# Maxima over partitions by a DRAM row, outputs in the raw weights' buffer, weights bounded and split by whole chunks

## Chip, core and metric

The kernel runs on one core of one Trainium2 chip. The metric is the device time of one execution in microseconds; of several runs of a kernel the median counts.

## What is computed

```python
# q, k, v: 8 batches x 8 heads x 576 positions x 64, float32
scores = scale * np.matmul(q, k.transpose(0, 1, 3, 2))
mask = pos[:, None] // 64 >= pos[None, :] // 64        # causal by blocks of 64
scores = np.where(mask, scores, -1000000000.0)
attn = np.exp(scores - np.max(scores, axis=-1, keepdims=True))
attn = attn / (np.sum(attn, axis=-1, keepdims=True) + 1e-09)
x = np.matmul(attn, v)                                 # then heads side by side: 4608 x 512
h = x @ w_in                                           # 512 x 2048
g = h * np.clip(h + 3.0, 0.0, 6.0) / 6.0
out = g @ w_out                                        # 2048 x 512
```

## The kernel before

Attention goes by slots: slot n is batch n // 4 and the pair of heads n % 4, so there are 32 of them. The second part (FFN below) goes by pieces of 384 or 192 tokens, 13 in all, and each piece by 16 rows f of 128 hidden features: `ffn1` makes the products `h` (24 half-width products where the piece has 384 tokens), ACT and DVE turn them into `r` and `g`, and three rows later `ffn2` adds the products `o` (18) to up to three accumulators of 128 tokens. After row 15 each accumulator is scaled into an `osb` tile and stored. Slots 0 to 3 and piece 0 work in float32. All others split each float32 operand into a high and a low float16 part and sum three products (`h`, `o`, `pv`) or two (`s`).

Splitting needs a power of two near the largest magnitude of the operand: per slot for q and k (`mb_q`), per batch for v, per chunk for the weights (8 chunks `c` of 256 hidden features, both matrices). `pow2_scale` finds it. Each partition first has its own bound (`mx`). With `exact`, PE spreads it along a row (`mt`), DVE takes the maximum (`dg`), PE spreads that over all partitions (`mb`), and DVE reads it (`am`, `pw`, `rs`). `v_max` does this for batch b before its slots (`vm1`), `w_max` for chunk c. `w_split` then writes high and low parts (`hi`, `lo`) in half chunks. The float32 form of chunk c lies where the split form of chunk c + 1 will be.

Weights arrive as 64-bit words in `raw` (one buffer of 4 KB per partition, besides parts of `ph` and other tiles) and are shortened to float32 with two `stage` tiles. `stage` has four buffers; `r` of pieces 1 to 12 and every `osb` take theirs from it too.

All instructions go through a `Recorder`, which is why they show one line in the profile (491). It notes what each reads and writes, and a planner orders them: each operation has a key (a due time, from tables such as `AT` for slots and `FT` for pieces, less `ADV` for attention on PE), each engine takes the ready operation with the lowest key, and readiness and costs are the planner's own estimates. Where `scaled` names several engines ("AVP"), the planner picks one. The engines then run their lists in that order, waiting where data is late. DMAs are all issued by SP, in one list: loads, stores, and transposes (`qkT`, `pT`) that turn split operands for PE. What stands behind a waiting DMA on SP waits too.

Of the kernel before, what the change touches and what calls it, by code (L numbers as in the profile page):

```python
# [25 lines left out]
U = 1.592
AS = (6.899, 12.918, 18.225, 24.115)
AL = 17.759
PV0 = 2.584
TA, TR, PR = 2.701, 5.502, 1.15  # L30
QR = 2.616
PVA, PVB = 1.013, 0.991
# [11 lines left out]
QL = -3.431
VL = -2.484
W0, WD = 16.803, 2.29
S0, SD = 55.334, 4.109
M0, MD = 36.221, 7.195
RT = (29.488, 39.58, 49.409, 59.423)
RS, RL, VL1 = 2.209, 24.843, 24.11  # L50
VM0, VMX = 49.529, 0.186
AT = ((4, 86.25), (6, 123.23), (8, 163.76), (9, 178.32), (10, 200.46), (12, 251.25), (14, 297.48), (15, 319.97), (16, 344.82), (24, 581.69), (32, 825.86))
FT = ((0, 34), (1, 120), (2, 165.28), (3, 233.86), (4, 274.28), (5, 355.06), (7, 504.5), (10, 755.22), (13, 989.58))
UNI = False
QP = 0.558
VP = 0.387
BLK = 64
EXPONENT_BITS = 0x7F800000

# [19 lines left out]
        return call  # L79


ADV = {("tensor", "a"): 99.24}
# [412 lines left out]
def kernel(  # L495
# [65 lines left out]
    def pow2_scale(mx, n, nm, to=None, exact=False):  # L561
# [8 lines left out]
        if exact:  # L570
            pt_ = ps_s.tile([P, 512], F32, tag="s", name=f"mt_{nm}")
            nc.joint = "mt", nm
            for h in range(2):
                wide = mx[:, h % n:h % n + 1].to_broadcast([P, BLK])
                nc.tensor.matmul(pt_[h * BLK:(h + 1) * BLK, :P], wide, ident, start=True, stop=True)
            nc.joint = None
            dg = sm.tile([P, n + 1], F32, tag=f"dg{n}", name=f"dg_{nm}")
            nc.vector.tensor_reduce(dg[:, n:], pt_[:, :P], axis=AX.X, op=ALU.max)
            nc.vector.tensor_scalar_mul(dg[:, :n], ident[:, :(n - 1) * BLK + 1:BLK], dg[:, n:])
            mx = dg[:, :n]  # L580
        ps = ps_s.tile([P, 512], F32, tag="s", name=f"mb_{nm}")
        nc.joint = "mb", nm
        for h in range(2):
            nc.tensor.matmul(ps[h * BLK:(h + 1) * BLK, :n], ones[:, :BLK], mx, start=True, stop=True)
        nc.joint = None
        nc.vector.tensor_scalar_max(am, ps[:, :n], TINY)
# [52 lines left out]
    def w_load(w, c, half):  # L639
# [35 lines left out]
            op0=ALU.logical_shift_left, op1=ALU.bitwise_or,  # L675
        )

    def w_max(c):

        acc = sm.tile([P, 2, 2], F32, tag="wacc", bufs=2, name=f"wacc{c}")  # L680
        for wi, w in enumerate("io"):
            for half in range(2):
                c32 = w_f32(w, c, half)
                ab = ffp.tile([P, WC], F32, tag="stage", bufs=NST_B, name=f"ab{w}{c}_{half}")
                ab = ab.rearrange("p (r l n) -> p r l n", r=c32.shape[1], l=2)
                nc.scalar.activation(ab, c32, AF.Abs, accum_out=acc[:, wi, half:half + 1])
# [4 lines left out]
    def w_split(c):

        rs = rsio[:, c]
        for wi, w in enumerate("io"):
            for half in range(2):
                c32 = w_f32(w, c, half)
                part = w_part(w, c, half)
                hi, lo = (part[:, :, i].rearrange("p r (l n) -> p r l n", l=2) for i in range(2))
# [829 lines left out]
```

## Time and profile before

| | before |
|---|---|
| median of 3 runs | 985.28 us (984.22 to 986.99) |
| profiled execution, its time | 982.83 us |
| profiled execution, its span | 981.0 us |
| granted TensorE clock | 0.999 |
| PE busy | 964.2 us (98%) |
| DVE busy | 756.4 us (77%) |
| ACT busy | 696.5 us (71%) |

The profile page gives busy time by engine. The view by stages gives it for stretches of the span (us from its start); the view of waits says for which instruction an engine stood idle and who released it. PEld is the loading of weights into PE, which overlaps the products. A line of groups gives count, busy time, mean ns of one, and idle time before it.

### The profile page before, as it was taken

How to read it: one execution, taken by the hardware profiler on the slowest of the kernel's cores; microseconds unless marked ns; L12 is line 12 of the kernel's file. 1: busy time of each engine (PE TensorE's matmuls, PEld its weight loads, DVE VectorE, ACT ScalarE, POOL GpSimd, SP SyncE). 2: the span in 40 equal slices, each digit the busy share in tenths (PEclk: the TensorE clock that was granted, in tenths of full speed). 3: DMA queues.
4: the chain of work that ended last, by engine and by line, in shares of the span. 5: the costliest groups of instructions: out<-in, count | busy, mean ns of one | idle time of the engine just before them, and what ended most of it. 6: DMA issues, size and time to landing. Idle time of an engine off the chain costs nothing.

```text
span 981.0 us, 29087 instructions
## 1 busy us (share of the span) xinstructions
PE 964.2 (98%) x11754; PEld 722.9 (74%) x11754; DVE 756.4 (77%) x2081; ACT 696.5 (71%) x1840; POOL 28.3 (3%) x109
## 2 busy tenths in 40 slices
PE   8999999999999999999999999999999999999998
PEld 6655447877778867777777677777777777777776
DVE  6889998999989999999999898899886432332331
ACT  6899789778778888888878788787775433333332
POOL 3012000000000000000000000000000000000000
PEclk9999999999999999999999999999999999999999
DMA  6966689899898899898899898786664200000000
GB/s 141 277 204 223 159 154 178 169 183 189 155 173 148 149 175 157 170 162 148 161 186 177 151 188 156 132 164 131 108 133 77 36 34 1 1 33 1 34 2 33
DMA packets 414199, 128.91 MB, mean 131 GB/s; under 512 B 403184, under 2 KB 403440, under 8 KB 414064
## 3 DMA queue, kind: packets, MB, share of 16 engines
q1 hardware_dynamic: 414064, 127.05, 66.5%
q8 instruction: 92, 1.51, 0.6%
q14 instruction: 43, 0.35, 0.1%
HBM read 45.09 MB, written 9.44 MB: 56 GB/s over the span
## 4 chain that ended last, share of the span: by engine, by line
PE 58%; DVE 6%; DMA 2%; ACT 1%; issue 1%; DVEq 0%; ACTq 0%
PE o L491 25%; PE h L491 25%; PE s L491 4%; PE pv L491 4%; DMA pT<-ph 2%; DVE st L491 1%; DVE phl L491 1%; DVE ph L491 1%; DVE r L491 1%; DVE g L491 1%; DVE qks L491 1%; DVE vhl L491 0%; ACT p L491 0%; DVE x L491 0%; ACT r L491 0%
## 5 line engine op out<-in xcount | busy, mean ns | idle before, releaser
L491 PE MATMUL h<-x,win 128*64 128x384 f16 (+3 forms) x4790 | 440.7, 319 | 4.4 <-DVE r L491 4.4
L491 PE MATMUL o<-wout,g 128*64 128x512 f16 (+2 forms) x3424 | 432.3, 383 | 0.0
L491 PEld LDWEIGHTS <-win 128*64 128x64 f16 x4608 | 296.1, 110 | 62.5 <-issue 6.5
L491 PEld LDWEIGHTS <-g 128*64 128x64 f16 x3264 | 219.2, 110 | 91.6
L491 ACT ACTIVATE r<-h,eg,sh 128x192 f32<-128x192 f32 (+1 forms) x240 | 134.1, 580 | 115.2 <-PE h L491 110.8
L491 DVE SCALAR_TENSOR_TENSOR r<-r,eg,h 128x384 f32<-128x384 f32 (+1 forms) x192 | 110.3, 575 | 132.0 <-ACT r L491 131.3
L491 ACT ACTIVATE p<-s,st,esc 128x64 f32<-128x64 f32 (+1 forms) x280 | 163.1, 586 | 13.6 <-DVE ph L491 7.3
L491 DVE SCALAR_TENSOR_TENSOR g<-r,g 128x384 f16<-128x384 f32 (+1 forms) x192 | 99.5, 519 | 34.1 <-ACT g L491 33.3
L491 DVE TENSOR_REDUCE st<-s 128x1 f32<-128x64 f32 (+1 forms) x280 | 119.2, 446 | 6.9 <-PE s L491 6.1
L491 ACT ACTIVATE g<-r 128x384 f16<-128x384 f32 (+1 forms) x157 | 77.4, 494 | 59.2 <-DVE r L491 58.7
L491 PE MATMUL s<-qkT 128*64 128x64 f16 (+7 forms) x1120 | 101.8, 287 | 1.9 <-ACT p L491 1.3
L491 PEld LDWEIGHTS <-vhl 128*64 128x64 f16 x1680 | 74.0, 110 | 13.5 <-issue 4.1
L491 PEld LDWEIGHTS <-qkT 128*64 128x64 f16 x1120 | 62.0, 110 | 23.5 <-issue 7.6
L491 PE MATMUL pv<-pT,vhl 128*64 128x192 f16 (+2 forms) x1680 | 74.4, 233 | 1.9 <-DMA pT<-ph 0.9
L491 DVE SCALAR_TENSOR_TENSOR ph<-p,st,ph 128x256 f16<-128x256 f32 (+2 forms) x168 | 66.5, 444 | 0.1
L491 DVE SCALAR_TENSOR_TENSOR phl<-p,st,phl 128x512 f16<-128x512 f32 (+1 forms) x84 | 62.8, 789 | 0.3 <-ACT phl L491 0.3
L491 ACT ACTIVATE st<-st,esc 128x1 f32<-128x1 f32 (+2 forms) x127 | 36.8, 291 | 34.3 <-DVE st L491 32.9
L491 ACT ACTIVATION_READ_ACCUMULATOR p<-s,st,esc 128x1 f32 x280 | 55.0, 196 | 0.0
L491 ACT ACTIVATE ph<-p,st 128x64 f16<-128x64 f32 (+5 forms) x106 | 43.2, 450 | 15.8 <-DVE st L491 14.2
L491 DVE SCALAR_TENSOR_TENSOR qks<-qk,rs_q,qks 128x576 f16<-128x576 f32 x56 | 44.5, 807 | 0.1
L491 ACT ACTIVATE qks<-qk 128x576 bf16<-128x576 f32 x56 | 37.8, 677 | 0.3 <-DMA qkT<-qks 0.3
L491 ACT ACTIVATE x<-pv 128x192 f16<-128x192 f32 (+1 forms) x56 | 20.3, 363 | 11.5 <-PE pv L491 10.0
(150 smaller groups left out, 847.0 us busy)
## 6 DMA issues: line engine op xcount, KB each, us to landing
out_dram<-osb SPq DMA_DIRECT2D x35, 256.0 KB, 2.7
vnat<-in_v_dram SPq DMA_DIRECT2D x64, 128.0 KB, 3.0
qk<-in_q_dram SPq DMA_DIRECT2D x28, 288.0 KB, 3.4
qk<-in_k_dram SPq DMA_DIRECT2D x28, 288.0 KB, 4.3
rawi<-in_moe_w_in_dram SPq DMA_DIRECT2D x8, 512.0 KB, 4.5
rawo<-in_moe_w_out_dram SPq DMA_DIRECT2D x8, 512.0 KB, 4.7
ph<-in_moe_w_in_dram SPq DMA_DIRECT2D x6, 512.0 KB, 4.8
ph<-in_moe_w_out_dram SPq DMA_DIRECT2D x6, 512.0 KB, 4.0
```

What stands on the lines that cost most here:

```text
L491: getattr(eng, method)(*args, **kw)
```

## The change

Six edits go together. `pow2_scale` has a second way (`far`) for chunks 3 to 7 and batches 1 to 7: the partitions' bounds are stored to a row in DRAM, read back with the row repeated on every partition (`al`), and reduced by DVE. `w_max` takes one sum of magnitudes over a whole chunk of a matrix in place of the larger of two sums over halves, and the scale of `g` leaves two more powers of two for that. `w_split` works on whole chunks, on ACT and DVE alone. The first two `osb` tiles of a piece share one tile with tag `raw`; the third stays in `stage`. The last `osb` is scaled and stored in two halves, stored by SP and ACT. k of slot 0 is loaded by ACT. The planner's tables are new.

```diff
-AT = ((4, 86.25), (6, 123.23), (8, 163.76), (9, 178.32), (10, 200.46), (12, 251.25), (14, 297.48), (15, 319.97), (16, 344.82), (24, 581.69), (32, 825.86))
+AT = ((4, 86.25), (6, 123.58), (8, 163.76), (9, 178.32), (10, 199.99), (12, 251.29), (13, 269.94), (14, 285.67), (15, 306.89), (16, 332.72), (24, 569.88), (32, 807.78))
+WFAR, VFAR = 3, 1
...
-ADV = {("tensor", "a"): 99.24}
+ADV = {("tensor", "a"): 19.74}
...
-            if self.on_chip(a):
+            if self.on_chip(a) or a.tensor.name.startswith("dr_"):
...
-    E_G = 2.0 ** -27
+    E_G = 2.0 ** -25
...
+    drp = ctx.enter_context(tc.tile_pool(name="dr", bufs=2, space=bass.MemoryType.DRAM))
...
+        if exact and far:
+            row = drp.tile([n, P], F32, tag=f"row{n}", name=f"dr_row_{nm}")
+            nc.sync.dma_start(row.rearrange("n p -> p n"), mx)
+            al = sm.tile([P, n, P], F32, tag="al", bufs=1, name=f"al_{nm}")
+            nc.sync.dma_start(
+                al.rearrange("p n x -> p (n x)"),
+                row.rearrange("n p -> (n p)").rearrange("(o x) -> o x", o=1).to_broadcast([P, n * P]),
+            )
+            nc.vector.tensor_reduce(am, al, axis=AX.X, op=ALU.max)
+            nc.vector.tensor_scalar_max(am, am, TINY)
...
     def w_max(c):
-        acc = sm.tile([P, 2, 2], F32, tag="wacc", bufs=2, name=f"wacc{c}")
+        acc = sm.tile([P, 2], F32, tag="wm", name=f"wm{c}")
         for wi, w in enumerate("io"):
-            for half in range(2):
-                c32 = w_f32(w, c, half)
...
-                nc.scalar.activation(ab, c32, AF.Abs, accum_out=acc[:, wi, half:half + 1])
...
+            c32, _ = w_whole(w, c)
...
+            nc.scalar.activation(ab, c32, AF.Abs, accum_out=acc[:, wi:wi + 1])
+        pow2_scale(acc, 2, f"w{c}", (pwio[:, c], rsio[:, c]), exact=True, far=c >= WFAR)
...
-                nc.scaled(hi, c32, rs[:, wi:wi + 1], "AVP")
...
+            nc.scaled(hi, c32, rs[:, wi:wi + 1], "AV")
...
-            vscale[b] = pow2_scale(m1, 1, f"v{b}", exact=True)
+            vscale[b] = pow2_scale(m1, 1, f"v{b}", exact=True, far=b >= VFAR)
...
-                nc.sync.dma_start(
+                (nc.sync if n or not s else nc.scalar).dma_start(
...
-            o = ffp.tile([P, DM], F32, tag="stage", bufs=NST_B, name=f"osb{pc}_{t}")
+            if t == 0:
+                pair = ffp.tile([P, 2, DM], F32, tag="raw", bufs=1, name=f"osb{pc}")
+            o = pair[:, t] if t < 2 else ffp.tile([P, DM], F32, tag="stage", bufs=NST_B, name=f"osb{pc}_{t}")
...
+            if pc == NPC - 1 and t == nt - 1:
+                for h, e in enumerate((nc.sync, nc.scalar)):
+                    cs = slice(h * DM // 2, (h + 1) * DM // 2)
+                    nc.scaled(o[:, cs], a[:, cs], so[:, t:t + 1], "AV")
+                    e.dma_start(rows[:, cs], o[:, cs])
+                continue
```

What it does to the order, at three places. SP's list at slot 17, where batch 5's maximum falls in the new order; before, first:

```order
L491 DMA vnat3_103<-in_v_dram 64x2x64
L491 DMA_TRANSPOSE pT17_1_1378<-phl17_6_1386 128x8x128
L491 DMA_TRANSPOSE pT17_1_1378<-phl17_7_1387 128x8x128
L491 DMA_TRANSPOSE pT17_1_1378<-phl17_8_1388 128x10x128
L491 DMA_TRANSPOSE pT18_0_1397<-ph0_87 128x8x128
```

And now:

```order
L495 DMA vnat3_105<-in_v_dram 64x2x64
L495 DMA dr_row_v5_1481<-vm1_5_1477 128x1
L495 DMA_TRANSPOSE pT17_1_1339<-phl17_6_1347 128x8x128
L495 DMA_TRANSPOSE pT17_1_1339<-phl17_7_1348 128x8x128
L495 DMA_TRANSPOSE pT17_1_1339<-phl17_8_1349 128x10x128
L495 DMA al_v5_1482<-dr_row_v5_1481 128x128
L495 DMA_TRANSPOSE pT18_0_1360<-ph0_89 128x8x128
```

The row's store stands ahead of the three transposes of slot 17 and the broadcast read behind them. On DVE, `am_v5` then stands 13 rows behind `vm1_5`.

ACT's list where piece 2 ends and piece 3 has begun, before (`osb2_1` went to DVE):

```order
L491 ACTIVATE r3_2_955<-h3_2_954,eg_625,sh1_792 128x192
L491 ACTIVATE osb2_0_958<-o2_0_806,so2_957 128x512
L491 ACTIVATE g3_2_956<-r3_2_955 128x192
L491 ACTIVATE p11_6_1029,st11_2_1024<-s11_2_1_0_1027,st11_2_1024,esc11_939 128x448
L491 ACTIVATE p11_8_1030,st11_2_1024<-s11_2_1_0_1027,st11_2_1024,esc11_939 128x64
L491 ACTIVATE osb2_2_960<-o2_2_808,so2_957 128x512
L491 ACTIVATE p11_8_1030,st11_2_1024<-s11_2_1_1_1028,st11_2_1024,esc11_939 128x512
L491 ACTIVATE r3_3_973<-h3_3_972,eg_625,sh1_792 128x192
L491 ACTIVATE st11_2_1024<-st11_2_1024 128x3
L491 ACTIVATE g3_3_974<-r3_3_973 128x192
L491 ACTIVATE phl11_7_1032<-p11_7_1026,st11_2_1024 128x4x128
L491 ACTIVATE r3_4_980<-h3_4_979,eg_625,sh1_792 128x192
```

And now:

```order
L495 ACTIVATE r3_2_936<-h3_2_935,eg_605,sh1_783 128x192
L495 ACTIVATE vhl12_1033<-vnat2_104,rs_v3_1014 128x5x128
L495 ACTIVATE g3_2_937<-r3_2_936 128x192
L495 ACTIVATE osb2_939<-o2_1_797,so2_938 128x512
L495 ACTIVATE osb2_2_940<-o2_2_798,so2_938 128x512
L495 ACTIVATE p11_6_991,st11_2_986<-s11_2_1_0_989,st11_2_986,esc11_900 128x448
L495 ACTIVATE r3_3_948<-h3_3_947,eg_605,sh1_783 128x192
L495 ACTIVATE p11_8_992,st11_2_986<-s11_2_1_0_989,st11_2_986,esc11_900 128x64
L495 ACTIVATE p11_8_992,st11_2_986<-s11_2_1_1_990,st11_2_986,esc11_900 128x512
L495 ACTIVATE st11_2_986<-st11_2_986 128x3
L495 ACTIVATE r3_4_953<-h3_4_952,eg_605,sh1_783 128x192
```

The outputs stand at much the same place; of the three only `osb2_2` is still a tile of `stage`, and the `r3` tiles that follow it come from there too.

SP's list at the end of attention, before (slots 30 and 31 are the last):

```order
L491 DMA_TRANSPOSE qkT31_2124<-qks31_2118 128x27x128
L491 DMA_TRANSPOSE pT30_0_2106<-ph1_88 128x18x128
L491 DMA_TRANSPOSE pT30_1_2141<-phl30_6_2149 128x8x128
L491 DMA_TRANSPOSE pT30_1_2141<-phl30_7_2150 128x8x128
L491 DMA_TRANSPOSE pT30_1_2141<-phl30_8_2151 128x10x128
L491 DMA_TRANSPOSE pT31_0_2160<-ph0_87 128x8x128
L491 DMA_TRANSPOSE pT31_0_2160<-ph1_88 128x18x128
L491 DMA_TRANSPOSE pT31_1_2177<-phl31_6_2185 128x8x128
L491 DMA_TRANSPOSE pT31_1_2177<-phl31_7_2186 128x8x128
L491 DMA_TRANSPOSE pT31_1_2177<-phl31_8_2187 128x10x128
L491 DMA out_0_dram<-osb9_0_2052 128x512
```

And now:

```order
L495 DMA out_0_dram<-osb9_2025 128x512 x2
L495 DMA out_0_dram<-osb9_2_2026 128x512
L495 DMA_TRANSPOSE pT30_1_2085<-phl30_6_2093 128x8x128
L495 DMA_TRANSPOSE pT30_1_2085<-phl30_7_2094 128x8x128
L495 DMA_TRANSPOSE pT30_1_2085<-phl30_8_2095 128x10x128
L495 DMA_TRANSPOSE pT31_0_2103<-ph0_89 128x8x128
L495 DMA_TRANSPOSE pT31_0_2103<-ph1_90 128x18x128
L495 DMA_TRANSPOSE pT31_1_2127<-phl31_6_2135 128x8x128
L495 DMA_TRANSPOSE pT31_1_2127<-phl31_7_2136 128x8x128
L495 DMA_TRANSPOSE pT31_1_2127<-phl31_8_2137 128x10x128
L495 DMA out_0_dram<-osb10_2157 128x512 x2
```

The last eight transposes of attention stood ahead of piece 9's outputs and now stand behind them. In PE's list 4334 of 21630 rows stood behind the last `pv` product, and now 3134 of 21599 do.

More of the change, by code (lines that the diff above doesn't have):

```diff
@@ L24 @@
 WY = 27
[L26 to L32, printed above, removed]
+U = 1.625
+AS = (6.639, 12.914, 19.786, 24.055)
+AL = 10.368
+PV0 = 1.9
+TA, TR, PR = 2.701, 5.748, 1.464
+QR = 1.086
+PVA, PVB = 1.108, 1.726
 PHS = 18
@@ L38 @@
 EVR = 3
-EVP = 4
+EVP = 0
 PRO = True
 MEM = 0
+BIASV = 261.576
+WFAR, VFAR = 3, 1
 NMIN = 64
[L44 to L51, printed above, removed]
-AT = ((4, 86.25), (6, 123.23), (8, 163.76), (9, 178.32), (10, 200.46), (12, 251.25), (14, 297.48), (15, 319.97), (16, 344.82), (24, 581.69), (32, 825.86))
-FT = ((0, 34), (1, 120), (2, 165.28), (3, 233.86), (4, 274.28), (5, 355.06), (7, 504.5), (10, 755.22), (13, 989.58))
+QL = -2.821
+VL = -1.472
+W0, WD = 21.694, 2.383
+S0, SD = 59.569, 3.454
+M0, MD = 31.889, 6.545
+RT = (29.11, 39.473, 49.187, 59.325)
+RS, RL, VL1 = 1.999, 24.929, 36.728
+VM0, VMX = 83.864, 0.17
+AT = ((4, 86.25), (6, 123.58), (8, 163.76), (9, 178.32), (10, 199.99), (12, 251.29), (13, 269.94), (14, 285.67), (15, 306.89), (16, 332.72), (24, 569.88), (32, 807.78))
+FT = ((0, 34), (1, 120.0), (2, 165.17), (3, 233.57), (4, 272.17), (5, 348.85), (6, 404.53), (7, 499.08), (10, 740.5), (11, 837.37), (13, 980.62))
 UNI = False
-QP = 0.558
-VP = 0.387
+QP = 0.67
+VP = 0.437
 BLK = 64
@@ L97 @@
     LOADS = 95.0
-    BIAS = {"vector": 250.0, "gpsimd": 500.0}
     EDGE = 0.0
@@ L108, in __init__ @@
         self.adv = ADV
+        self.BIAS = {"vector": BIASV, "gpsimd": 500.0}
         for n in self.NAMES:
@@ L116, in box @@
     def box(a):
+        if not Recorder.on_chip(a):
+            return 0, 1, 0, 1
         sz = mybir.dt.size(a.dtype)
@@ L535 @@
     E_X = 2.0 ** -14
-    E_G = 2.0 ** -27
+    E_G = 2.0 ** -25
     C_EXP = (D ** -0.5) * 2.0 ** -28
     C_H = 2.0 ** -28
-    C_O = 2.0 ** -15 / 6.0
+    C_O = 2.0 ** -17 / 6.0
     TINY = 1e-18
@@ L559, with pow2_scale @@
     padded = []
-    def pow2_scale(mx, n, nm, to=None, exact=False):
+    def pow2_scale(mx, n, nm, to=None, exact=False, far=False):
         if to:
@@ L569, in pow2_scale @@
         am = sm.tile([P, n], F32, tag=f"am{n}", name=f"am_{nm}")
-        if exact:
-            pt_ = ps_s.tile([P, 512], F32, tag="s", name=f"mt_{nm}")
-            nc.joint = "mt", nm
+        if exact and far:
[8 more added lines that the diff above has]
+            nc.vector.tensor_scalar_max(am, am, TINY)
+        else:
+            if exact:
+                pt_ = ps_s.tile([P, 512], F32, tag="s", name=f"mt_{nm}")
+                nc.joint = "mt", nm
+                for h in range(2):
+                    wide = mx[:, h % n:h % n + 1].to_broadcast([P, BLK])
+                    nc.tensor.matmul(pt_[h * BLK:(h + 1) * BLK, :P], wide, ident, start=True, stop=True)
+                nc.joint = None
+                dg = sm.tile([P, n + 1], F32, tag=f"dg{n}", name=f"dg_{nm}")
+                nc.vector.tensor_reduce(dg[:, n:], pt_[:, :P], axis=AX.X, op=ALU.max)
+                nc.vector.tensor_scalar_mul(dg[:, :n], ident[:, :(n - 1) * BLK + 1:BLK], dg[:, n:])
+                mx = dg[:, :n]
+            ps = ps_s.tile([P, 512], F32, tag="s", name=f"mb_{nm}")
+            nc.joint = "mb", nm
@@ L573, in pow2_scale @@
             for h in range(2):
-                wide = mx[:, h % n:h % n + 1].to_broadcast([P, BLK])
-                nc.tensor.matmul(pt_[h * BLK:(h + 1) * BLK, :P], wide, ident, start=True, stop=True)
+                nc.tensor.matmul(ps[h * BLK:(h + 1) * BLK, :n], ones[:, :BLK], mx, start=True, stop=True)
             nc.joint = None
-            dg = sm.tile([P, n + 1], F32, tag=f"dg{n}", name=f"dg_{nm}")
-            nc.vector.tensor_reduce(dg[:, n:], pt_[:, :P], axis=AX.X, op=ALU.max)
-            nc.vector.tensor_scalar_mul(dg[:, :n], ident[:, :(n - 1) * BLK + 1:BLK], dg[:, n:])
@@ L580, in pow2_scale @@
[L580 to L586, printed above, removed]
+            nc.vector.tensor_scalar_max(am, ps[:, :n], TINY)
         nc.vector.tensor_scalar(
@@ L676, in w_load, with w_whole @@
         )
+    def w_whole(w, c):
+        if w == "i":
+            part = win[:, c]
+            c32 = win[:, c + 1].bitcast(F32) if c + 1 < NCH else None
+        else:
+            part = wout[:, 2 * c:2 * c + 2]
+            c32 = wout[:, 2 * c + 2:2 * c + 4].bitcast(F32) if c + 1 < NCH else None
+        if c32 is None:
+            t = flat(xb[2 if w == "i" else 3], F32)[:, :2 * WC]
+            c32 = t.rearrange("p (r l n) -> p r l n", r=part.shape[1], l=2)
+        return c32, part
     def w_max(c):
-        acc = sm.tile([P, 2, 2], F32, tag="wacc", bufs=2, name=f"wacc{c}")
+        acc = sm.tile([P, 2], F32, tag="wm", name=f"wm{c}")
         for wi, w in enumerate("io"):
-            for half in range(2):
-                c32 = w_f32(w, c, half)
-                ab = ffp.tile([P, WC], F32, tag="stage", bufs=NST_B, name=f"ab{w}{c}_{half}")
-                ab = ab.rearrange("p (r l n) -> p r l n", r=c32.shape[1], l=2)
-                nc.scalar.activation(ab, c32, AF.Abs, accum_out=acc[:, wi, half:half + 1])
-        m = sm.tile([P, 2], F32, tag="wm", name=f"wm{c}")
-        nc.vector.tensor_reduce(m, acc, axis=AX.X, op=ALU.max)
-        pow2_scale(m, 2, f"w{c}", (pwio[:, c], rsio[:, c]), exact=True)
+            c32, _ = w_whole(w, c)
+            ab = ffp.tile([P, WC], F32, tag="stage", bufs=NST_B, name=f"ab{w}{c}")
+            ab = ab.bitcast(BF16).rearrange("p (r l n) -> p r l n", r=c32.shape[1], l=2)
+            nc.scalar.activation(ab, c32, AF.Abs, accum_out=acc[:, wi:wi + 1])
+        pow2_scale(acc, 2, f"w{c}", (pwio[:, c], rsio[:, c]), exact=True, far=c >= WFAR)
     def w_split(c):
@@ L694, in w_split @@
         for wi, w in enumerate("io"):
[L695 to L698, printed above, removed]
-                nc.scaled(hi, c32, rs[:, wi:wi + 1], "AVP")
-                nc.vector.scalar_tensor_tensor(
-                    lo, c32, rs[:, wi:wi + 1], hi, op0=ALU.mult, op1=ALU.subtract
-                )
+            c32, part = w_whole(w, c)
+            hi, lo = (part[:, :, i].rearrange("p r (l n) -> p r l n", l=2) for i in range(2))
+            nc.scaled(hi, c32, rs[:, wi:wi + 1], "AV")
+            nc.vector.scalar_tensor_tensor(
+                lo, c32, rs[:, wi:wi + 1], hi, op0=ALU.mult, op1=ALU.subtract
+            )
     gs = []
@@ L1338, in ffn2_ @@
             n, half = min(w - t * P, P), w - t * P < P
-            o = ffp.tile([P, DM], F32, tag="stage", bufs=NST_B, name=f"osb{pc}_{t}")
+            if t == 0:
+                pair = ffp.tile([P, 2, DM], F32, tag="raw", bufs=1, name=f"osb{pc}")
+            o = pair[:, t] if t < 2 else ffp.tile([P, DM], F32, tag="stage", bufs=NST_B, name=f"osb{pc}_{t}")
             oc = o[:, :DM // 2] if half else o
             ac = a[:, :DM // 2] if half else a
+            rows = out[row + t * P:row + t * P + n]
+            if pc == NPC - 1 and t == nt - 1:
[4 more added lines that the diff above has]
+                continue
             nc.scaled(oc, ac, so[:, t:t + 1] if pc else 1.0 / 6.0, "AV")
-            rows = out[row + t * P:row + t * P + n]
             if half:
@@ L1431 @@
         t = RT[n]
-        at(t - QR, qk_load32_rest, n, lead=RL - QR)
-        at(t - QR, qk_prep32, n, 1)
+        at(t - max(QR, 0.0), qk_load32_rest, n, lead=RL - max(QR, 0.0))
+        at(t - max(QR, 0.0), qk_prep32, n, 1)
         at(AS[3] + 0.1 + 0.1 * n, v_max, n)
```

## Prediction

> **What bounds the kernel now.** I read the engine sums first, then the stages, then who waited for whom. The page:
>
> ```profile
> span 981.0 us, 29087 instructions
> PE 964.2 (98%) x11754; PEld 722.9 (74%) x11754; DVE 756.4 (77%) x2081; ACT 696.5 (71%) x1840; POOL 28.3 (3%) x109
> ```
>
> The view by stages (length, then busy us of PE, PEld, DVE, ACT, POOL):
>
> ```profile
> 0.00:20.00 20.00, 15.36 (x103) 12.24 (x104) 13.12 (x41) 12.81 (x42) 7.41 (x32) 1.00 0.65 147
> 60.00:120.00 60.00, 60.00 (x411) 29.50 (x409) 59.14 (x170) 52.38 (x129) 10.24 (x10) 1.00 0.70 195
> 120.00:280.00 160.00, 156.58 (x2172) 116.64 (x2170) 152.01 (x455) 134.00 (x372) 2.59 (x16) 1.00 0.93 167
> 280.00:360.00 80.00, 76.83 (x1220) 61.52 (x1213) 70.31 (x209) 66.53 (x186) 1.21 (x8) 1.00 0.94 166
> 360.00:740.00 380.00, 378.86 (x4980) 295.27 (x4978) 345.50 (x949) 305.64 (x830) 4.84 (x32) 1.00 0.85 154
> 740.00:970.00 230.00, 229.58 (x2542) 175.26 (x2539) 81.01 (x158) 86.36 (x172) 0.00 (x0) 1.00 0.10 22
> ```
>
> PE is never idle for long, and from 740 on it works alone: DVE is at 81 of 230. So whatever product is taken off PE anywhere earlier lets the last FFN products start earlier, one for one, while PE stays fed. PE's idle time is the other thing to win: 4.6 us at the start, 3.4 in 120:280, 3.2 in 280:360, 1.1 in 360:740, 0.4 after. DVE is nearly full in 120:280 (152 of 160), so a wait put on DVE there is the danger. The waits (total, times, longest):
>
> ```profile
> PE h L491 <- DVE r L491: 4.4, 3, 2.0
> PE pv L491 <- DMA pT<-ph: 0.9, 2, 0.5
> ACT r L491 <- DMA out_dram<-osb: 3.8, 1, 3.8
> DVE vmax L491 <- DMA vnat<-in_v_dram: 1.4, 3, 0.6
> ```
>
> **The products removed.** A maximum over partitions is mt, then dg on DVE, then mb, am. The timeline of PE at batch 2's:
>
> ```profile
> 201.04 0.41 PE L491 MATMUL mt_v<-ident,vm 128*64 128x128 f32 x4
> 201.26 0.68 PE L491 MATMUL h<-x,win 128*64 128x384 f16 x6
> 202.72 0.26 PE L491 MATMUL mb_v<-dg_v,one 128*64 128x1 f32 x4
> 202.81 1.17 PE L491 MATMUL h<-x,win 128*64 128x384 f16 x12
> ```
>
> Busy times overlap, so I take the step from one start to the next: 0.22 for mt, 0.09 for mb, 0.31 together. Twelve of them go (chunks 3 to 7, batches 1 to 7): -3.7. Ends: 0 if PE only waits instead, and -8.0 by busy time (12 x 0.67). The steps say -3.7. DVE loses a reduction and a product over dg and gains a reduction over al: about even, 0.
>
> **The outputs' buffer.** Where piece 2 ends, its three osb tiles sit in the four stage buffers that r needs too:
>
> ```profile
> 289.24 1.51 SPq L491 DMA_DIRECT2D out_dram<-osb  x3
> 293.07 0.51 ACT L491 ACTIVATE r<-h,eg,sh 128x192 f32<-128x192 f32 x1 [3.84 <-DMA out_dram<-osb]
> 293.61 0.41 DVE L491 SCALAR_TENSOR_TENSOR r<-r,eg,h 128x192 f32<-128x192 f32 x1 [3.14 <-ACT r L491]
> 294.08 1.18 PE L491 MATMUL h<-x,win 128*64 128x192 f16 x24 [2.03 <-DVE r L491]
> 298.83 0.68 PE L491 MATMUL s<-qkT 128*64 128x256 f16 x8 [1.09 <-ACT p L491]
> ```
>
> ACT stood 3.84 us for the store, PE 2.03 right behind it and 1.09 for ACT's backlog. In the ACT order of before the second r after the last osb (r3_4) takes the first osb's buffer. With one osb left in stage, counting four buffers round, that is r3_6, two products h and two o later (1.18 of h alone each), and the store has landed by then. -3.1; ends 0 (the stall comes back elsewhere) and -3.8 (all of ACT's stand). The pair buffer is free: raw weights are long split, and pieces end tens of us apart.
>
> **The start.** k of pair 0 is issued by ACT beside q on SP:
>
> ```profile
> 0.73 0.99 SPq L491 DMA_DIRECT2D qf<-in_q_dram  x2
> 1.76 1.02 SPq L491 DMA_DIRECT2D qf<-in_k_dram  x2
> 5.37 0.56 DVE L491 TENSOR_SCALAR qkf<-qt 64x384 f32<-64x384 f32 x1 [3.01 <-ACT qkf L491]
> 5.80 0.49 ACT L491 ACTIVATE qkf<-qt 128x384 f32<-128x384 f32 x1 [0.47 <-PE qt L491]
> 6.39 2.74 PE L491 MATMUL sf<-qkf 128*128 128x128 f32 x8 [0.63 <-ACT qkf L491]
> ```
>
> k comes 1.0 earlier, its copy (ending 6.29) is no longer last, DVE's half of q (ending 5.93) is: -0.4. Ends 0 and -1.0. The table load that ACT has at the start moves behind its DMAs and ends long before 4.85.
>
> **The end.** The last tile's copy is halved over ACT and DVE and stored by two queues:
>
> ```profile
> 976.05 1.98 ACT L491 ACTIVATE osb<-o,so 128x512 f32<-128x512 f32 x3 [4.60 <-PE o L491]
> L491 ACT ACTIVATE osb<-o,so x28: 472/687/710, 203.2 to 977.3; 128x512 f32<-128x512 f32 x27, 128x256 f32<-128x256 f32 x1
> DMA to landing us min/median/max: 2.0/2.7/5.0
> out_dram<-osb SPq DMA_DIRECT2D x4, 64.0 KB, 2.8
> ```
>
> A copy of 256 columns took 0.47 for 0.69, and a store of 64 KB lands no sooner than one of 256 KB: -0.2. Ends 0 and -0.4.
>
> **Weights by whole chunks.** ACT saves 16 sums and 16 starts, DVE 14 to 16 starts; eight copies leave POOL for ACT and DVE:
>
> ```profile
> L491 ACT ACTIVATION_READ_ACCUMULATOR abi<-win 128x1 f32 x14 | 2.9, 210 | 0.0
> L491 POOL TENSOR_SCALAR win<-win,rsio 128x512 f16<-128x512 f32 x5 | 5.5, 1103 | 34.8 <-PE h L491 14.3 <-DVE win L491 10.7 <-DVE rsio L491 9.9
> ```
>
> ACT gains at least 16 x 0.21 = 3.4 and takes most of eight copies: about even. All of it lies in 60:120 and just after, beside a PE that was busy 60.00 of 60. 0; ends -1 and +1. Should that cover go, DVE (59.14 of 60) is late next.
>
> **The new order.** The order changes everywhere. Its largest move: behind the last pv product stood 4334 of PE's rows, now 3134. A row f of FFN is 84 such rows (24 h and 18 o products, each with its load) and takes 3.9 us in the chain of waits:
>
> ```profile
> 967.53 1.95 PE h L491 x24
> 965.59 1.94 PE o L491 x18
> ```
>
> 1200/84 x 3.9 = 56 us: attention ends that much later beside PE's work, so DVE's 345.5 of 380 thin out to about 84% (345.5 + 56 x 81/230, over 436). At most the 1.1 us of 360:740 can go. The 3.4 idle in 120:280 are dealt anew: 0 to double. I take -1.0; ends -4.5 and +3.4.
>
> **The round trip through DRAM.** It adds 24 DMAs on SP: a row written, a wait for its landing on SP, a broadcast read; DVE waits for that at am. Tightest of the batches is 5: between row and read stand three transposes on SP, and 13 rows of DVE stand between vm1 and am (in the six others 25 to 38, some 10 us at 345.5/949 = 0.36 each and the waits between).
>
> ```profile
> 290.85 5.74 SPq L491 DMA_TRANSPOSE pT<-phl  x3
> L491 DVE SCALAR_TENSOR_TENSOR phl<-p,st,phl 128x512 f16<-128x512 f32 x56 | 39.7, 745 | 0.0
> L491 DVE SCALAR_TENSOR_TENSOR phl<-p,st,phl 128x640 f16<-128x640 f32 x28 | 24.6, 878 | 0.3 <-ACT phl L491 0.3
> L491 DVE SCALAR_TENSOR_TENSOR r<-r,eg,h 128x384 f32<-128x384 f32 x160 | 97.5, 609 | 127.2 <-ACT r L491 126.7
> L491 DVE SCALAR_TENSOR_TENSOR g<-r,g 128x384 f16<-128x384 f32 x160 | 88.5, 553 | 33.6 <-ACT g L491 32.8
> vnat<-in_v_dram SPq DMA_DIRECT2D x32, 32.0 KB, 3.0
> ```
>
> The third transpose needs phl of the 640 columns: g, two phl copies (0.5 each, an estimate below their products), 2 x 0.75, r, phl 0.88 are 4.5 us of DVE; its issue 1.9 (5.74/3), the read 3.0: 9.4. DVE comes to am after 4.5 and g, x, r, g and three short reductions, some 3 us: 7.5. So DVE stands about 1.9 there. The five chunks fall into the full stretch of DVE, so I count them with it as six tight places. The buffers swallow some of a stand (ACT's 3.84 cost PE 3.1), and in the old order DVE waited 1.4 in all for 96 loads of v. Between 0 and 6 x 1.9 = 11.4 I take +0.4, nearest to that row.
>
> Behind SP's wait stand transposes. The Trainium skill (DMA: Bandwidth & Descriptors, Anatomy of one DMA) says that a semaphore wait happens on the issuing sequencer before dispatch, the engines not waiting themselves. By that rule the read holds SP, and all behind it, until the row has landed; no row of before shows a DMA that waits for another's DRAM bytes. It is the third rival, and the sum by it would be the time given there.
>
> Sum: -3.7 - 3.1 - 0.4 - 0.2 - 1.0 + 0.4 = -8.0. The profiled execution took 982.83, so 974.8; the median of the runs is 985.28, 2.45 more, so **977.3**.
>
> **Rivals.** First, the stall moves: one osb still sits in stage and the new order pays the 3.1 and the 1.0 elsewhere. For it: 120:280 has 3.4 idle with no osb in it. Against: 3.8 was the only wait for osb. -3.9: 981.4.
>
> Second, slower: DVE waits at am. If reads land as late as the latest store (5.0 in place of 2.7), DVE stands 1.9 + 2.3 = 4.2 at each of the six tight places, and PE 3.4 by the ratio of the osb stall: 974.8 to 995.2, 997.7 against the median. It decides from 1.8 us of PE per place (11 in all: 8 to undo the gain, 3 to be seen). For it: DVE's 59.14 of 60. Against: 1.4 us of waits for 96 loads.
>
> Third, SP is held. Where one short DMA stands between row and read (chunks 4 and 6), SP stands 2.7 less its issue, about 2. If the transposes behind are that late in the seven batches and PE's pv stands 1.3 each: +9.1, 986.4. Against: PE waited for pT 0.9 in all.
>
> Fourth, more gain: all idle time of 120:740 but a remnant goes: -3.7 - 3.8 - 1.0 - 0.4 - 4.5 = -13.4, 971.9.
>
> **How the numbers follow.** Forecast 0.57, stall moves 0.15, DVE waits 0.08, SP held 0.07, more gain 0.13. 0.3% is 3.0 us, what the three runs (984.22 to 986.99) can tell from no change. Below 982.3: 0.57 + 0.13 + most of the first = 0.82; within: SP held and the rest of the first, 0.10; above: 0.08. The range runs from the fourth (971.5) to the first with half of 120:280's idle more (983).
>
> **What would show it.** mt and mb for three chunks and one batch only; no wait ACT r for osb of 3 us; sf at 6.0 for 6.39; the last osb half as long; in 360:740 DVE at 84% and PE idle under 1; waits DVE am for al under 4 us in all. The forecast is wrong if DVE's or PE's waits for DMA exceed 10, or if PE's idle in 120:360 grows over 6.6.

## The result and the profile after

The changed kernel took 1036.78 us (1035.07 to 1038.62, 4 runs), against 985.58 for the kernel before on the same chip: a ratio of 1.052 [1.0495, 1.0544], 51 us slower where 8 us less was forecast. Its profiled execution took 1037.43 us. Two executions that lie far outside the others of their kernel (1146.01 us of the run with the planner told the trip's length, 2620.99 us of the run with DVE's wait) are left out of the medians and ratios below, and why they took so long is open. The page after:

```profile
span 1035.6 us, 28740 instructions
PE 976.8 (94%) x11636; PEld 726.9 (70%) x11636; DVE 769.0 (74%) x2095; ACT 675.7 (65%) x1751; POOL 18.3 (2%) x101
PEclk9999898989998999999999999999999999999999
```

The trace has 118 products less on PE, and PE is busy 12.6 us longer; its idle time went from 16.8 us (981.0 - 964.2) to 58.8. The third row is the clock granted to PE: it falls below full in several slices of the first half. The stages, in the columns of the view shown for before:

```profile
60.00:120.00 60.00, 53.46 (x315) 26.04 (x313) 44.29 (x119) 41.07 (x83) 0.30 (x2) 0.97 0.81 160
120.00:280.00 160.00, 134.90 (x1700) 93.80 (x1702) 133.75 (x388) 112.73 (x306) 2.27 (x14) 0.93 0.87 149
280.00:360.00 80.00, 76.44 (x1188) 62.34 (x1186) 68.77 (x208) 60.49 (x169) 0.91 (x6) 0.96 0.97 153
360.00:740.00 380.00, 370.56 (x4730) 285.85 (x4728) 316.45 (x866) 270.33 (x724) 4.25 (x28) 1.00 0.81 140
```

Most of the idle time lies in 60:280 (31.6 us), where five chunks and the first batches go through DRAM. Who waited for what:

```profile
DVE am_v L495 <- DMA al_v<-dr_row_v: 24.1, 5, 7.7
DVE am_w L495 <- DMA al_w<-dr_row_w: 11.6, 4, 7.0
PE pv L495 <- DMA pT<-ph: 11.4, 3, 6.8
PE s L495 <- DMA qkT<-qks: 5.1, 1, 5.1
SPq L495 <- DMA dr_row_w<-wm: 22.0, 4, 6.7
SPq L495 <- DMA dr_row_v<-vm: 6.5, 1, 6.5
```

All three ways in which the trip could hurt are there at once: DVE stands at `am`, SP stands for the row to land, and PE waits for transposes. The place of batch 2 in the timeline, in order:

```profile
207.81 1.61 SPq L495 DMA_DIRECT2D dr_row_v<-vm  x1
217.32 1.18 SPq L495 DMA_DIRECT2D al_v<-dr_row_v  x1
224.01 0.29 DVE L495 TENSOR_REDUCE am_v<-al_v 128x1 f32<-128x128 f32 x1 [6.86 <-DMA al_v<-dr_row_v]
224.51 1.49 PE L495 MATMUL o<-wout,g 128*64 128x512 f16 x6 [4.67 <-DVE g L495]
```

The row of 512 bytes is issued at 207.81 and its read not before 217.32; DVE stands 6.86 us, PE 4.67 for the `g` that stands behind `am` on DVE. And the DMA view (count, KB each, median us from issue to landing):

```profile
al_w<-dr_row_w SPq DMA_DIRECT2D x5, 128.0 KB, 4.9
al_v<-dr_row_v SPq DMA_DIRECT2D x7, 64.0 KB, 5.0
dr_row_w<-wm SPq DMA_DIRECT2D x5, 1.0 KB, 11.1
```

A store of 1 KB landed after 11.1 us (the trace holds the landing of one of the five), where the third rival priced a row at 2.7 and the forecast's sum has no term for it.

### The profile page after: what moved, and what is told of

It is laid out like the page before. It is cut to its first block, busy times and chain, and to the rows that moved or that the text cites. A ratio compares the mean times of both kernels' runs of the same rounds, so it can differ in the third digit from the quotient of the medians.

```text
span 1035.6 us, 28740 instructions
## 1 busy us (share of the span) xinstructions
PE 976.8 (94%) x11636; PEld 726.9 (70%) x11636; DVE 769.0 (74%) x2095; ACT 675.7 (65%) x1751; POOL 18.3 (2%) x101
## 5 line engine op out<-in xcount | busy, mean ns | idle before, releaser
L495 PE MATMUL h<-x,win 128*64 128x384 f16 (+3 forms) x4786 | 432.7, 321 | 4.4 <-DVE g L495 3.5
L495 PEld LDWEIGHTS <-g 128*64 128x64 f16 x3264 | 223.2, 111 | 103.1 <-DVE g L495 4.9
L495 ACT ACTIVATE g<-r 128x384 f16<-128x384 f32 (+1 forms) x138 | 68.0, 493 | 80.7 <-DVE r L495 80.6
L495 DVE TENSOR_REDUCE st<-s 128x1 f32<-128x64 f32 (+1 forms) x280 | 114.5, 447 | 7.7 <-PE s L495 7.3
L495 PE MATMUL s<-qkT 128*64 128x64 f16 (+7 forms) x1120 | 94.2, 291 | 17.6 <-DVE x L495 7.8
L495 PE MATMUL pv<-pT,vhl 128*64 128x192 f16 (+2 forms) x1680 | 76.1, 237 | 17.8 <-DMA pT<-ph 11.4
L495 DVE SCALAR_TENSOR_TENSOR ph<-p,st,ph 128x256 f16<-128x256 f32 (+3 forms) x168 | 67.0, 445 | 0.0
L495 ACT ACTIVATE st<-st,esc 128x1 f32<-128x1 f32 (+2 forms) x111 | 32.0, 290 | 50.7 <-DVE st L495 50.0
L495 ACT ACTIVATE ph<-p,st 128x256 f16<-128x256 f32 (+5 forms) x102 | 41.6, 450 | 28.1 <-DVE st L495 14.4
```

Source lines behind the costliest of these rows:

```text
L495: getattr(eng, method)(*args, **kw)
```

## The experiments

"Before" is the kernel before, timed beside the others on the same chip: 985.65, 984.81, 985.40, 985.09, 985.61 and 985.65 us in the six groups of runs. A number from 0.99 to 1.08 is the ratio to it, with the 95% interval behind it.

**No trip, and the trip's DMAs by themselves.** All maxima on PE again; late in the kernel three trips that no product needs: a row of one maximum (piece 10, with the last three transposes of attention behind it), of two (piece 11), and a 64 KB tile (piece 12), the last two where PE works alone.

```diff
-WFAR, VFAR = 3, 1
+WFAR, VFAR = 8, 8
...
+nc.sync.dma_start(row.rearrange("n p -> p n"), src)   # n = 1, 2; then a 128 x 512 B tile
```

> The changed kernel with every maximum over partitions on PE (no round trip for chunks or batches), all else as changed; and, late in pieces 10 to 12, three round trips that nothing needs: 128 pieces of 4 bytes (piece 10), 256 pieces of 4 bytes (piece 11), 128 pieces of 512 bytes (piece 12), the last two after attention, when no transposes are in flight. Theory A, the round trip is the cause: DVE's 35.7 us of waits for al go, PE's idle time falls from 58.8 to some 20 and the granted clock returns to 0.999, so 970 to 990. Theory B, the new order and tables are slow by themselves: still above 1015. For the trips: if a store of 4-byte pieces is slow by itself, it lands after 8 us or more also in the quiet stretch and the 512-byte one after 2 to 3; if the queue's load made it slow, all land within 3.

987.85 us, 1.0028 [1.0013, 1.0043]. So the trip costs 49 of the 51 us, and the other edits with the new tables together gain nothing. The probes:

```profile
dr_row_p<-pq SPq DMA_DIRECT2D x1, 0.5 KB, 7.5
dr_row_p<-pq SPq DMA_DIRECT2D x1, 1.0 KB, 7.8
dr_row_p<-g SPq DMA_DIRECT2D x1, 64.0 KB, 1.5
```

The store of a row of two maxima takes 7.8 us with no transpose left in flight; 64 times its bytes, in pieces of 512 bytes, take 1.5. The row is slow by itself, not because of the queue it stands in.

**The trip on POOL's queue.**

```diff
-nc.sync.dma_start(row.rearrange("n p -> p n"), mx)
+nc.gpsimd.dma_start(row.rearrange("n p -> p n"), mx)     # and the read of al
```

> The changed kernel with both DMAs of each round trip issued by POOL in place of SP, so that the wait for the row's landing holds POOL, which has nothing else to do, and no transposes behind it. If SP's hold (28.5 us of waits for a row) carries the loss, below 1000. If DVE's wait for al carries it, DVE still waits 25 us or more and the time stays above 1015.

1050.99 us, 1.0676 [1.0628, 1.0723]: slower still. Now POOL stands where SP stood, and PE waits for transposes all the same, though nothing on SP waits for a row any more:

```profile
POOL al_v L495 <- DMA dr_row_v<-vm: 48.2, 5, 10.8
PE s L495 <- DMA qkT<-qks: 11.8, 2, 8.9
```

That SP is held by a row is then not what makes the transposes late.

**The planner told the trip's true length** (row 7.5 us longer, read 2 us), so that DVE comes to `am` later.

```diff
+if args[0].tensor.name.startswith("dr_"):
+    tail += 7500.0
+elif args[1].tensor.name.startswith("dr_"):
+    tail += 2000.0
```

> The changed kernel with the planner told that a row's store ends 7.5 us and its read 2 us later than it assumes; the same instructions, ordered anew. If the loss is that the order counts on a trip of some 6 us while it takes 13, DVE's waits for al fall below 5 us, SP's waits for rows below 8, and the time is 970 to 990. If trips hurt in another way (their load on the queue, or the tables), above 1010.

1036.61 us, 1.0533 [1.0504, 1.0561]; I expected most of the loss to go. DVE's waits for `al` did go, from 35.7 us to 3.4, SP's waits for rows too, from 28.5 us to 0.2, and the time stayed:

```profile
DVE am_w L499 <- DMA al_w<-dr_row_w: 3.4, 2, 2.3
PE s L499 <- DMA qkT<-qks: 8.6, 2, 6.7
PE pv L499 <- DMA pT<-ph: 8.1, 2, 7.1
SPq L499 <- DMA dr_row_w<-wm: 0.2, 1, 0.2
```

So DVE's wait, my second rival and then my theory, is not the carrier, and SP's, the third rival, is not either; what is left is the stores and reads themselves, or the order, which is new here.

**The trip alone, in the kernel before** (its tables, nothing else of the change; the edit is `far` in `pow2_scale`).

> The kernel before with the round trip alone (chunks 3 to 7, batches 1 to 7), its own tables and all else kept. Theory A: DVE waits for al 20 us or more, 1010 to 1035. Theory B: within 5 us of before, 980 to 990.

1057.35 us, 1.0751 [1.0722, 1.078]. The trip needs no help from the other edits. My theory from here on: the store of 4-byte pieces occupies the DMA engines, and what stands behind it is late.

The next four runs build the trip up in the kernel before, with the maxima still made and used on PE. PE's rows stay those of before, one by one, so no difference here is one of PE's order.

**The 12 stores alone, read by nobody.**

```diff
+if far:
+    row = drp.tile([n, P], F32, tag=f"row{n}", name=f"dr_row_{nm}")
+    nc.sync.dma_start(row.rearrange("n p -> p n"), mx)
```

> The kernel before, maxima still on PE, plus the 12 stores of a row to DRAM (128 or 256 pieces of 4 bytes each) that nothing reads; PE's order of instructions is the one of before, row by row. Pieces theory (the store of so many 4-byte pieces occupies the DMA engines and makes the transfers queued behind it late): most of the loss is here, 1010 to 1035 us. Hold theory (SP standing at the store until the maximum is there is what costs): 990 to 1010, and the same with large pieces. Waits theory (only DVE's wait for the row's way back costs): 984 to 989.

1031.74 us, 1.0463 [1.0441, 1.0484]: +46.9 us for 12 stores of 0.5 or 1 KB that nothing waits for.

**The same stores with 512-byte pieces.** The maximum is one column of a tile of 128 columns, and the whole tile is stored.

```diff
+    row = drp.tile([P, P], F32, tag="rowd", name=f"dr_row_{nm}")
+    nc.sync.dma_start(row, wides[...])
```

> As the run with the 12 unread rows, but each store moves 128 pieces of 512 bytes (the whole tile in which the maximum is one column); same place, same wait of SP, same order on PE. Pieces theory: 984 to 990. Hold theory: as the run with the 4-byte pieces, 990 to 1010. Waits theory: 984 to 989.

985.76 us, 1.001 [0.9996, 1.0024]. Place, wait of SP for the maximum and order are the same; only the pieces differ, and with them the bytes (64 KB each).

**The way back, and DVE's wait**, each on top of the run before it.

```diff
+    nc.sync.dma_start(al.rearrange("p n x -> p (n x)"), row...to_broadcast([P, n * P]))   # first run
+    nc.vector.tensor_reduce(pm[:, :n], al, axis=AX.X, op=ALU.max)                          # second run
```

> The 12 rows stored in 4-byte pieces and read back to all partitions, SP standing at each read until its row has landed; no engine uses what is read; same order on PE. Pieces theory: 0 to 12 us above the run with the unread rows (SP holds the transposes and loads behind it for the row's 7 to 12 us, but these were late already). Hold theory: 15 to 40 above the run with unread rows, about 1015 to 1030. Waits theory: 984 to 992.

> As the run before it, and DVE reduces what is read (into a tile that nothing uses), so DVE also waits for the row's way back; same order on PE. Pieces theory: 3 to 15 us above the run whose read nobody uses, about 1020 to 1045. Hold theory: the same small step. Waits theory: the whole loss is here, 1020 to 1045, after three runs near 986.

1043.40 us, 1.0579 [1.0558, 1.06], and 1047.64, 1.0634 [1.0607, 1.0661]. The steps are 46.9 for the stores, 11.7 for the reads and SP's hold, 4.2 for DVE's wait (5.4 by the ratios): the pieces carry most, and each of the other two a little.

**What it is about the pieces.** First, the same 4-byte pieces, each 512 bytes from the next in DRAM:

```diff
-row = drp.tile([n, P], F32, tag=f"row{n}", name=f"dr_row_{nm}")
-nc.sync.dma_start(row.rearrange("n p -> p n"), mx)
+row = drp.tile([P, n, P], F32, tag=f"row{n}", name=f"dr_row_{nm}")
+nc.sync.dma_start(row[:, :, 0], mx)
```

> The kernel before plus the 12 unread rows of 4-byte pieces, but each piece to a place of its own, 512 bytes apart in DRAM, instead of all beside each other in one row; PE's order as before. If the number or size of the pieces is what costs: 1015 to 1040, as the row did (1031.7). If it is that many pieces are written into the same few hundred bytes of DRAM: 984 to 995.

984.98 us, 1.0001 [0.9992, 1.001]. Nothing is left of the loss, with as many pieces of the same size. The Trainium skill (DMA: Bandwidth & Descriptors, Specifications) says that below 512 bytes a transfer misses line rate and the engine reads, modifies and writes; that alone would make these as slow as the row's, and they are not. What differs is where they lie: the row puts 128 pieces into the same 512 bytes. Then pieces of 64 bytes without a gap, and pieces of 4 bytes 64 bytes apart:

```diff
+nc.sync.dma_start(row, wides[...][:, :16])           # row [P, 16]: 64-byte pieces
```

> As the run with 128 pieces of 512 bytes, with 128 pieces of 64 bytes that fill 8 KB of DRAM without a gap; PE's order as before. If any piece under 512 bytes is slow to write: 1015 to 1040. If only pieces that share a short stretch of DRAM with others are slow, or only such of a few bytes: 984 to 992.

```diff
+row = drp.tile([P, n, 16], F32, tag=f"row{n}", name=f"dr_row_{nm}")   # 4 bytes of every 64
```

> As the run whose 4-byte pieces lie 512 bytes apart, with the pieces 64 bytes apart, so that eight of them share 512 bytes; PE's order as before. If pieces disturb each other only within the same few dozen bytes: 984 to 987. If within the same 512 bytes: some loss, 990 to 1025, by how far eight neighbours are from the row's 128.

985.63 us, 1.0004 [0.9995, 1.0013], and 985.64, 1.0004 [0.9995, 1.0014]. So neither the size of a piece nor a distance of 64 bytes costs anything by itself. Eight of these pieces lie in 512 bytes, where the row has 128: whether the distance to the neighbour counts or the number in a short stretch these runs do not separate, and distances between 4 and 64 were not tried. The DMA view of the row (one landing of the seven and one of the five are in the trace), of the pieces 512 bytes apart and of those 64 apart:

```profile
dr_row_v<-vm SPq DMA_DIRECT2D x7, 0.5 KB, 8.3
dr_row_w<-wm SPq DMA_DIRECT2D x5, 1.0 KB, 10.1
```

```profile
dr_row_v<-vm SPq DMA_DIRECT2D x7, 0.5 KB, 2.5
dr_row_w<-wm SPq DMA_DIRECT2D x5, 1.0 KB, 4.0
```

```profile
dr_row_v<-vm SPq DMA_DIRECT2D x7, 0.5 KB, 2.8
dr_row_w<-wm SPq DMA_DIRECT2D x5, 1.0 KB, 3.5
```

How 8 us of a store that nobody waits for become PE's time is seen where the two kernels run the same list. SP's list at batch 4, with the pieces 512 bytes apart:

```profile
351.54 0.57 SPq L494 DMA_DIRECT2D dr_row_v<-vm  x1
...
354.49 5.25 SPq L494 DMA_TRANSPOSE qkT<-qks  x1
359.84 3.44 SPq L494 DMA_TRANSPOSE pT<-ph  x1
```

and with the row, and who waited in the end:

```profile
379.56 0.57 SPq L494 DMA_DIRECT2D dr_row_v<-vm  x1
...
382.52 12.26 SPq L494 DMA_TRANSPOSE qkT<-qks  x1
394.87 2.90 SPq L494 DMA_TRANSPOSE pT<-ph  x1
396.92 0.85 PE L494 MATMUL s<-qkT 128*64 128x64 f16 x12 [4.69 <-DMA qkT<-qks]
```

Between row and transpose stand the loads of the next q and k. The transpose takes SP 12.26 us in place of 5.25, everything behind it moves by as much, and PE stands 4.69 for `qkT`. The same stretch of PE's list, 5 us long, by the row and by the spaced pieces (last column: GB/s moved by the DMAs):

```profile
385.00:390.00 5.00, 5.00 (x66) 3.29 (x64) 3.90 (x10) 4.10 (x11) 0.00 (x0) 1.00 1.48 64
```

```profile
357.00:362.00 5.00, 5.00 (x66) 3.27 (x64) 3.90 (x10) 4.12 (x11) 0.00 (x0) 1.00 1.40 205
```

The DMA engines are as busy by the share beside it (1.48 and 1.40, the time that packets were under way over that of 16 engines), and move 64 GB/s in place of 205. The single packets of the two traces tell more. The row's own pieces take 9 ns each at most and all start within 0.3 us, in both runs. Of the 256-byte packets that start in these 5 us half take 18 ns or less in both, but with the row there are 1215 of them in place of 3903, and the longest takes 5.8 us in place of 1.2. So my theory was half right: the pieces do not keep the DMA engines busy themselves, but some packets of what stands behind them stand for microseconds.

**The change with a row of few pieces.** DVE turns each 32 x 32 block of the column, and a maximum's row goes out as 4 pieces of 128 bytes.

```diff
+nc.vector.transpose(sq, mx)                  # mx widened to 32 columns, zeros behind
+for i in range(n):
+    nc.sync.dma_start(row[i].rearrange("(c x) -> c x", c=4), sq.rearrange("(c q) x -> c q x", c=4)[:, i])
-nc.sync.dma_start(row.rearrange("n p -> p n"), mx)
```

> The changed kernel with its row moved in few pieces: DVE turns the column of maxima into rows of 32 values, and the row goes to DRAM as 4 pieces of 128 bytes per maximum instead of 128 of 4 bytes; the way back, SP's waits and DVE's reduction are unchanged. Pieces theory: nearly all of the loss goes, 984 to 996 us (987.9 without any trip, less 3.7 of products, plus DVE's waits and a read that holds SP for 3 to 5 us). Rival (what costs is that anything is sent through DRAM and waited for): 1015 to 1040.

986.05 us, 1.0007 [0.9998, 1.0017]. The round trip itself can be afforded: SP stands 4.6 us in all for rows, and DVE no longer for `al`. The run is some 2.5 us shorter than that without any trip (1.0032, below); as the order differs too, this does not show what the removed products are worth.

**Why the rest gained nothing.** The outputs' buffer alone in the kernel before, first as the planner orders it, then with the planner told that these tiles still take stage buffers, so that PE's rows stay those of before:

```diff
+if t == 0:
+    pair = ffp.tile([P, 2, DM], F32, tag="raw", bufs=1, name=f"osb{pc}")
+o = pair[:, t] if t < 2 else ffp.tile([P, DM], F32, tag="stage", ...)
...
+self.meta[tn] = ("stage", 4) if osb else ...      # second run only
```

> The kernel before with the outputs alone moved into the raw weights' buffer (a pair of two tiles, none on the stage buffers that ACT's r needs). Forecast's term: ACT's wait for the outputs' stores goes, and with it 3.1 us: 981 to 984. Rival (the stall moves to the next wait, as DVE or PE is the limit there): 985 to 987.

> The kernel before with the outputs in the raw weights' buffer, as in the run that moved them alone, but with the planner kept to the order of the kernel before: PE's rows are those of before, one by one. If the forecast's term of 3.1 us is right and it was the new order that took it back: 981.5 to 983.5. If the stall moves to the next wait whatever the order: 985 to 987.

987.07 us, 1.0018 [1.0009, 1.0026], and 981.60, 0.997 [0.9957, 0.9983]. The same edit is worth -3.5 us in one order and +1.7 in another. In the second PE goes on where it had stood 2.03 and 1.09 before:

```profile
292.13 1.19 PE L494 MATMUL h<-x,win 128*64 128x192 f16 x24
295.59 0.68 PE L494 MATMUL s<-qkT 128*64 128x256 f16 x8
```

In the first it stands at batch 2's first slot instead, 90 us earlier:

```profile
204.92 0.85 PE L491 MATMUL s<-qkT 128*64 128x64 f16 x12 [2.59 <-DMA qkT<-qks]
208.10 0.64 PE L491 MATMUL s<-qkT 128*64 128x256 f16 x4 [1.33 <-DVE am_q L491]
```

The stretch 200:210 of the planner's order, then of the order of before:

```profile
200.00:210.00 10.00, 5.47 (x74) 4.64 (x72) 8.07 (x33) 7.90 (x23) 0.00 (x0) 0.72 1.00 194
```

```profile
200.00:210.00 10.00, 8.37 (x132) 7.23 (x129) 8.82 (x32) 7.92 (x24) 0.00 (x0) 1.00 1.22 213
```

PE is busy 5.47 of 10 us, at a granted clock of 0.72, against 8.37 at 1.00.

The change without any trip, and that with the first k on SP again:

```diff
-WFAR, VFAR = 3, 1
+WFAR, VFAR = 8, 8
...
-(nc.sync if n or not s else nc.scalar).dma_start(      # second run only
+nc.sync.dma_start(
```

> The changed kernel with all maxima on PE, so without any trip through DRAM: what the other edits are worth together. By the forecast's terms (outputs -3.1, start -0.4, end -0.2, order -1.0): 980.5. By the run with the probes in the tail: 987 to 988.

> The run without any trip, with the first k back on SP behind q. By the forecast's term (two queues gain 0.4): 0.4 above that run. By the trace of the changed kernel (PE's first transpose 0.8 us and its first score 1.1 us later): 0.8 to 1.5 below it, 986 to 987.

988.04 us, 1.0032 [1.0019, 1.0045], and 987.92, 1.0033 [1.002, 1.0047]. The five other edits and the new tables lose 3 us together; where k is loaded makes no difference that can be measured.

Two tries for a better version: the change with few pieces and k on SP, and the kernel before with the outputs' buffer and few pieces.

> The changed kernel with its row in 4 pieces of 128 bytes and with the first k back on SP: the best of the change as far as the runs show it. 984.5 to 985.5, if the start's 1.1 us adds to the run with few pieces (986.05); 986 or more if the start is hidden.

> The kernel before (its tables, its halves of chunks, its start and end) with the outputs in the raw weights' buffer, the planner told that they take the stage buffers, and the maxima of later chunks and batches through DRAM in 4 pieces of 128 bytes. If the two gains add and the order stays good: 977.5 to 980 (981.6, less some 2.5 for the products, as between the runs with and without few pieces). If the planner, which now places 24 groups of products less, falls into an order with a stall as it did with the outputs alone: 983 to 989.

985.14 us, 1.0005 [0.9996, 1.0013], which cannot be told from the run with few pieces, and 987.48, 1.002 [1.0011, 1.0029]. In the second the planner, with products gone, again makes an order that stands around 200 us, and the gain of the outputs' buffer is lost once more:

```profile
206.89 0.75 PE L497 MATMUL s<-qkT 128*64 128x64 f16 x12 [3.34 <-DMA qkT<-qks]
```

The best kernel of the study is the one with the outputs' buffer alone under the old order, 981.60 us.

## Why the prediction was wrong

**The round trip (+0.4 forecast, about +49 measured).** The step that failed is what the trip was counted by: DVE's stand at `am`, the engine that needs the result, between 0 and 11.4 us. What the stores do to the DMAs behind them was put at nothing, and no row of before showed such a store. Twelve stores that nobody waits for cost 46.9 us by what stands behind them. The row's landing was no term of the sum either: in the tightest place it is taken to lie behind three transposes, and only the third rival prices it, at 2.7 us, the median of the outputs' stores of 256 KB. The row has 128 or 256 pieces of 4 bytes side by side, and took 7.5 and 7.8 us late in the kernel and 11.1 (256 pieces) in the middle of things. The signs that the prediction gave for being wrong are all there: DVE's and PE's waits for DMAs over 10 us (35.7 and 16.5), and PE's idle time in 120:360 at 28.7 (25.1 + 3.6) against 6.6. Two slips in the working change nothing here: the fourth rival is 971.9 by its sum and 971.5 in the range, and the second rival's price is added to a sum that holds the +0.4 for the same wait.

**The rivals.** DVE's wait at `am` came as described and far larger (35.7 us in all), and is still not the cause: without it (3.4) the time is the same, and on top of stores and reads it adds 4 to 5. SP's hold was forecast as +9.1. SP did stand, 28.5 us for rows, in agreement with the sentence that the prediction cites from the Trainium skill (DMA: Bandwidth & Descriptors, Anatomy of one DMA). Hold and reads together add 11.7 in the order of before, and with SP's waits gone (0.2) the time is the same. Neither rival named the transfers behind the stores. The first rival, that the stall moves, is what the outputs' buffer alone shows under the planner's order; of the fourth, more gain, nothing shows.

**The products (-3.7).** Not shown by themselves: the nearest are two ratios (1.0007 and 1.0032, 2.5 us apart) of kernels whose order differs, each uncertain by about 1 us. By the count they went as forecast: `mt` and `mb` of three chunks and one batch are left, 96 of the 118 products less (the other 22 are missing in the run without the trip too).

**The outputs' buffer (-3.1).** Right in place, mechanism and size: -3.5 with the order held. ACT's 3.84 for the store is gone.

**The new order (-1.0; ends -4.5 and +3.4).** Wrong in sign, and outside its ends: with the outputs alone the order costs 5.2 (+1.7 against -3.5); in the change without the trip, 988.04 stands 7.5 above the 980.5 that the remaining terms made. The forecast treated the order as a term of its own that keeps the others whole; it can take each back. Attention did thin out much as forecast: in 360:740 of the run without the trip DVE is busy 326.54 of 380 us, 86% for 84 (345.50, 91%, before). That bought nothing, as PE is idle there 1.2 us, for 1.1 before.

**Start (-0.4) and end (-0.2).** By the trace both are wrong, by time they are nil. In the changed kernel PE waits for k first, 4.74 us against 3.9 for q before, and the first score starts at 7.51, where it was 6.39 before and 6.0 forecast:

```profile
4.74 1.51 PE L495 MATMUL qt<-ident,qf 128*128 128x128 f32 x6 [4.74 <-DMA qf<-in_k_dram]
7.51 1.83 PE L495 MATMUL sf<-qkf 128*128 128x128 f32 x6 [1.26 <-POOL qkf L495]
1032.51 0.48 DVE L495 TENSOR_SCALAR osb<-o,so 128x256 f32<-128x256 f32 x1 [5.81 <-ACT osb L495]
```

The last row shows the end: DVE's half of the last output ran after ACT's half, so halving saved no time: from the start of the last 72 products to the end it is 11.7 us before (969.29 to 981.0) and after (1023.94 to 1035.6). Why two halves of one tile ran in turn was not tried.

**Whole chunks (0).** Not tried alone; inside the 3 us that the five edits and the tables lose together.

## What to carry to other kernels

Before a few hundred values go from a column to a row through DRAM, count the pieces and look how they lie: 128 or 256 pieces of 4 bytes side by side cost the kernel some 4 us each time, the same pieces 64 bytes apart, or a row that DVE had turned into 4 pieces, nothing that could be measured. Price a DMA not only by who waits for it but by what is queued behind it. And where a planner makes the order, test an edit with the order held: here one edit was worth -3.5 us with it and +1.7 without.

## What was not expected of the hardware

Pieces of 4 bytes stored next to each other land after 8.3 us (128) and 10.1 (256, one store of each), with 64 bytes between their starts after 2.8 and 3.5; what in the chip holds them, and the packets behind them, no run shows.

After PE has stood, its granted clock is lower for some us, so a stand costs more than its length. In the run with the 12 unread rows (columns as before; the clock is the third from the end):

```profile
140.33:143.75 3.42, 1.30 (x12) 0.53 (x11) 3.42 (x9) 3.39 (x9) 0.45 (x2) 1.00 0.46 81
143.00:145.00 2.00, 0.43 (x4) 0.43 (x6) 2.00 (x5) 1.76 (x6) 0.00 (x0) 0.69 0.98 206
145.00:150.00 5.00, 5.00 (x20) 1.64 (x18) 3.64 (x15) 2.87 (x6) 0.32 (x2) 0.50 1.03 189
```

The first row is the stretch before the clock falls; then PE is busy 0.43 of 2 us, and 5.00 of 5 at half the clock. The Trainium skill (TensorE: Matmul & The Clock Gate, What's actually happening) says that the clock is halved after an idle window of about 3.4 us and full again after a busy one. The 0.50 agrees, and so do the lengths: the halved stretches of this run last 3.41 or 6.83 us. But the 3.42 us before this one were not idle, as PE was busy 1.30 of them. The lower clock is part of the loss: with the products of before in the order of before, PE is busy 978.9 us in this run against 964.2, 14.7 of the 47 us. In the changed kernel PE is busy 12.6 us longer with fewer products.
